# Attention scores as two float32r products on full rows, with operands split once per pair of heads

## The chip, the cores and the metric

The kernel runs on one core of one Trainium2 chip. The metric is device time in microseconds (us) of one execution. A core has a matrix engine (TensorE, PE in the profile; its weight loads are shown apart as PEld), a vector engine (VectorE, DVE), an engine for functions of one input (ScalarE, ACT), GpSimd (POOL) and SyncE (SP), which here only issues transfers. They run beside each other and wait for each other by semaphores. Data lies in SBUF (128 partitions); matrix products land in PSUM, 8 banks of 512 float32 a partition.

## The reference

Attention over 8 batches, 8 heads, 576 positions and 64 features a head, in which only scores within tau of their row's maximum count, then a feed-forward network (FFN) whose activation is a rational function:

```python
scores = scale * np.matmul(q, k.transpose(0, 1, 3, 2))           # 576 x 576 a head
thresh = np.max(scores, axis=-1, keepdims=True) - tau
scores = np.where(scores >= thresh, scores, -1000000000.0)
scores = scores - np.max(scores, axis=-1, keepdims=True)
attn = np.exp(scores)
attn = attn / (np.sum(attn, axis=-1, keepdims=True) + 1e-09)
x = np.matmul(attn, v)                       # heads side by side: 4608 x 512
h = x @ w_in                                 # 512 x 2048
g = (a0 + a1*h + a2*h**2 + a3*h**3) / (1 + |b0|*|h| + |b1|*h**2 + 1e-6)
out = g @ w_out                              # 2048 x 512
```

Which scores count depends on small differences between them, so the scores have to be nearly exact in float32.

## The kernel before

**Units.** Heads are taken in pairs, two times 64 features filling the 128 partitions: 32 pairs (8 batches of 4). 576 positions are four blocks of 128 and a rest of 64. A pair has four full units (one block of 128 queries, both heads) and one short unit (the last 64 queries of both heads in one tile), 160 units in all. For each unit `unit_ops` makes these steps: score product (`f_qk`, lines 642 and 653, TensorE), row maximum (`f_max`, 663, VectorE), threshold (`f_thr`, 667, VectorE), a Prelu with a slope of 2^100 below the threshold (`f_pre`, 680, ScalarE), exponential with its sum (`f_sum`, 684, ScalarE), reciprocal (693 and 697, VectorE), a split of the result into two float16 parts (`f_hi`, 278 or 280; `f_lo`, 708), two DMA transposes issued by SP (720), the product with V (733, TensorE), and the split of its result into `xh` and `xl` (741 or 743, and 747). Since `BY_ACT` is `(1, (0,))`, every unit takes this way; the other branch in the code (`f_exp`, `f_mask`) is not used.

**The score product.** Q and K are in float32, with the features on the partitions. Q is loaded into `QQ` by three transfers and K into `KK` by two (`load_ops`, on SP), two tiles of each in turn, and Q is scaled once a pair ("qs", 278 or 280). Head 0 uses partitions 0 to 63, head 1 partitions 64 to 127. `product` (642) multiplies 64 rows by 512 keys for one head; the last 64 keys of both heads come from 653, over all 128 rows, where blocks of zeros keep the heads apart. In the profile one float32 product of the code is two MATMUL instructions, each with its own weight load.

**The FFN.** `moe_ops` takes 256 rows by 512 hidden columns at a time: a first product in float16 parts (845), ScalarE's scaled copy (854), a chain of VectorE and ScalarE steps for the rational function (859 to 899), and a second product in float32 (906). Its steps of one batch lie between the attention units of the next; those of the last batch follow the last unit.

**Weights.** They arrive as 64-bit words by 32 transfers on the POOL queue (452, 487), each behind a small POOL instruction (400) that waits until the transfer three before it has landed, and are decoded by VectorE and ScalarE (`decode_ops`).

**Order of the work.** Each step is an `Op` with its engine or a choice of engines (`FLEX`), a cost in us, a key (its due place in units), and `Hold`s on buffers. `Plan.order` plays the queues forward with these costs and takes the steps in the order in which they start; that order is the program of each queue. "DMA" stands for SP's queue, "GD" for POOL's. Buffers of one pool are granted in the order of rank. The plan books each buffer, but which physical buffer a step gets is left to the tile pools (`sb.tile(... tag=..., bufs=...)`), which go round in order of request. `POOLS` gives their numbers: "t" are 4 KB work tiles a partition, for weights and the FFN. PSUM banks 0 to 5 hold scores in pairs of banks for the first 25 units (`SINGLE`, one head each), after that banks 0 to 2 hold both heads. While the plan sees TensorE idle early on, it puts in small products that keep it warm (1035).

Of the kernel before, what the change touches and what calls it, by code (L numbers as in the profile page):

```python
# [23 lines left out]
POOLS = {"e": 3, "hi": 3, "pT": 2, "st": 6, "sc": 2, "t": 12, "u": 4, "x": 4, "xr": 1}  # L24
# [4 lines left out]
LEAD, LEAD0 = 2.88, 0.04  # L29
# [10 lines left out]
BY_ACT = (1, (0,))  # L40
# [10 lines left out]
FLEX = {"f1": {"ACT": 0.66, "DVE": 0.345}, "f6": {"DVE": 0.62}, "s1": {"ACT": 0.65, "DVE": 0.396}, "qs": {"ACT": 0.7, "DVE": 0.42},  # L51
        "s2": {"DVE": 0.66},
        "vmax": {"ACT": 0.58, "DVE": 0.68}, "thr": {"DVE": 0.155},
# [24 lines left out]
class Hold:  # L78
# [3 lines left out]
    def __init__(self, pool, uses, sets=None):  # L82
        self.pool, self.uses, self.until, self.sets, self.bank = pool, uses, 0.0, sets, None


class Plan:
# [3 lines left out]
    LAT = {"PE": 0.27, "ACT": 0.28, "DVE": 0.22, "POOL": 0.16, "DMA": 2.3, "GD": 3.4}  # L90
    OWN = {"PE": 0.0, "ACT": 0.15, "DVE": 0.13, "POOL": 0.1, "DMA": 2.3, "GD": 3.4}
# [8 lines left out]
    def pool(self, name, n):  # L100
        self.pools[name] = [0.0] * n
# [8 lines left out]
    def spot(self, h, t):  # L110

        if h.sets is None:
            slots = self.pools[h.pool]
            return (min(slots), None) if slots else None
# [14 lines left out]
    def order(self):  # L129
# [20 lines left out]
        while left:  # L150
# [41 lines left out]
            for h in o.take:  # L192
                if h.sets is None:
                    slots = self.pools[h.pool]
                    slots.remove(min(slots))
                else:
                    h.bank = self.spot(h, t)[1]
                    for i in h.bank:
                        self.banks[i] = None
                if h.pool in line:  # L200
                    line[h.pool].pop()
            for h in o.drop:
# [5 lines left out]
                elif not h.uses:  # L208
                    self.pools[h.pool].append(h.until)
# [18 lines left out]
def masked_attention_rational_ffn(  # L228
# [16 lines left out]
    P = 128  # L245
# [16 lines left out]
    sb = ctx.enter_context(tc.tile_pool(name="sb", bufs=2))  # L262
# [25 lines left out]

    def bank(h):
# [17 lines left out]
    QW = S + REM  # L307
    NQ = 2
    QQs = [const.tile([P, QW], F32, name=f"QQ{i}") for i in range(NQ)]
    KKs = [const.tile([P, QW], F32, name=f"KK{i}") for i in range(NQ)]  # L310
    for t in QQs:
        nc.gpsimd.memset(t[:, NT * P:], 0.0)
    for t in KKs:
        nc.gpsimd.memset(t[0:D, 0:REM], 0.0)
        nc.gpsimd.memset(t[D:P, S:], 0.0)
# [18 lines left out]
    def scale_ops(key, get, up, inv, s, after, tag):  # L334
# [3 lines left out]
        plan.rank = key  # L338

        def f1():  # L340
            sc = small.tile([P, 4], F32, name=f"sc{tag}", tag="sc", bufs=POOLS["sc"])
# [3 lines left out]
        def f2():  # L345

            box["d"] = sb.tile([P, WS], F32, name=f"dg{tag}", tag="u", bufs=POOLS["u"])[:, 0:P]
# [15 lines left out]
        h, hd, hb = Hold("sc", 1), Hold("u", 1), Hold("b", 1, B1)  # L363
# [26 lines left out]
    def decode_ops(i, key, load, hold, dst=None):  # L390
# [13 lines left out]
        def f1():  # L404


            box["w"] = sb.tile([P, WS], F32, name=f"wt{i}", tag="u", bufs=POOLS["u"])
# [21 lines left out]
        l = op("GD", 2.7, key - 2.0, ld, (), [hold])  # L429
# [13 lines left out]
    for i in range(NW):  # L443
        pieces = []
        for c in range(NC):
# [3 lines left out]
            def load(n=n, c=c, i=i):  # L449
                rw = sb.tile([P, 2, WS], F32, name=f"rwi{n}", tag="t", bufs=POOLS["t"]).rearrange("p a b -> p (a b)")  # L450
                rw = words(rw)
# [30 lines left out]
    for f in range(NF):  # L482
        hold = Hold("t", 1)

        def load(f=f):
            rw = words(sb.tile([P, 2, WS], F32, name=f"rwo{f}", tag="t", bufs=POOLS["t"]).rearrange("p a b -> p (a b)"))
# [30 lines left out]
    def load_ops(bp):  # L517
# [3 lines left out]
        before = qk_done.get(bp - NQ, [])  # L521
        KK, QQ = KKs[bp % NQ], QQs[bp % NQ]
        first = bp == 0

        queue, eng = nc.sync, "DMA"

        def ldq():
            queue.dma_start(QQ[0:D, 0:S], qT[bb, pr, :, 0:S])
            queue.dma_start(QQ[D:P, 0:NT * P], qT[bb, pr, :, S + REM:])
            queue.dma_start(QQ[D:P, S:], qT[bb, pr, :, S:S + REM])  # L530

        def ldk():
            queue.dma_start(KK[0:D, REM:], kT[bb, pr, :, 0:S])
            queue.dma_start(KK[D:P, 0:S], kT[bb, pr, :, S:2 * S])

        lq = op(eng, 1.6, p - (4.6 if first else 4.0), ldq, before)
        lk = op(eng, 1.1, p - (4.5 if first else 3.9), ldk, before)
        k_done[bp] = [lk]
        q_done[bp] = [op(FLEX["qs"], 0, p - 1.3, lambda: times(QQ, QQ, qscale), [lq])]

    def load_v_ops(bp):
# [13 lines left out]
        def mx():  # L555
# [4 lines left out]
            else:  # L560
                jk = sb.tile([P, WS], F32, name=f"vj{bp}", tag="u", bufs=POOLS["u"])
                nc.scalar.activation(jk.bitcast(BF16)[:, 0:NT * P + 2 * D], t, AF.Abs, accum_out=vms[bb][:, pr:pr + 1])
# [33 lines left out]
    def x_tile(ck):  # L596
        if ck not in xt:
            tag, n = ("x", POOLS["x"]) if ck[0] == "m" else ("xr", POOLS["xr"])
            xt[ck] = tuple(sb.tile([P, NP, CT], F16, name=f"{tag}{s}{ck[1]}_{ck[2]}", tag=tag + s, bufs=n) for s in "hl")
        return xt[ck]  # L600

    def unit_ops(bp, t):
# [4 lines left out]
        by_act = (bp * (NT + 1) + t) % BY_ACT[0] in BY_ACT[1]  # L607
        heads = (0, 1) if full else (0,)
        QQ, KK = QQs[bp % NQ], KKs[bp % NQ]
# [14 lines left out]
        def f_qk(h2s):  # L624
            if not full:
                h2s = [None]
            s, dst = {}, {}
            for hh in h2s:
                b0, b1 = sh[hh or 0].bank[0], sh[hh or 0].bank[-1] + 1
                s[hh] = ps[:, b0:b1, :].rearrange("p b k -> p (b k)")  # L630
                if hh:

                    s[hh] = s[hh][:, (b1 - b0) * 512 - S:]
                    dst[hh] = s[hh][:, REM:S], s[hh][:, 0:REM]
                else:
                    s[hh] = s[hh][:, 0:S]
                    dst[hh] = s[hh][:, 0:NT * P], s[hh][:, NT * P:S]
                box["s"][hh or 0] = s[hh]

            def product(hh, k0, k1, dst, **kw):  # L640
                r, c0 = (slice(0, P), NT * P) if hh is None else (slice(hh * D, (hh + 1) * D), t * P)
                nc.tensor.matmul(dst, QQ[r, c0:c0 + P], KK[r, k0:k1], **kw)  # L642

            one = dict(start=True, stop=True)
            rests = (S, QW), (0, REM)
            for hh in h2s:

                product(hh, REM, S, dst[hh][0], **one)
            if len(h2s) == 2:

                for hh in h2s:
                    k0, k1 = rests[hh]
                    nc.tensor.matmul(dst[hh][1], QQ[:, t * P:(t + 1) * P], KK[:, k0:k1], **one)  # L653
            elif full:
                product(hh, *rests[hh], dst[hh][1], **one)
            else:
                product(hh, *rests[0], dst[hh][1], start=True, stop=False)
                product(hh, *rests[1], dst[hh][1], start=False, stop=True)

        def f_max(hh):  # L660
            if hh == 0:
                box["st"] = small.tile([P, 8], F32, name=f"st{name}", tag="st", bufs=POOLS["st"])
            nc.vector.tensor_reduce(box["st"][:, hh:hh + 1], box["s"][hh], AX.X, ALU.max, negate=True)  # L663

        def f_thr(h0, h1):
            if by_act:
# [411 lines left out]
```

## Time and profile before

| | us |
|---|---|
| three runs | 1463.76, 1470.2, 1471.97 (median 1470.2) |
| profiled execution | 1455.38 |
| its span, first to last instruction | 1453.6 |
| TensorE busy | 1395.0 |
| VectorE busy | 1230.0 |
| ScalarE busy | 1114.5 |
| POOL busy | 31.5 |

The mean granted clock of TensorE is 0.973 of full speed. Rows of the profile name a line of the kernel, an engine, an operation and its tiles (out<-in, buffer numbers left out), the shapes, and the count. "Mean ns" is the time of one instruction; matrix products overlap, so their pace is read from the distance between starts and not from it. "Idle before" is the time in which the engine stood still just ahead of such an instruction, with what released it ("issue" where the profile shows no cause).

### The profile page before, as it was taken

What the parts mean: (1) busy time and instruction counts of PE and PEld (TensorE: products, weight loads), DVE (VectorE), ACT (ScalarE), POOL (GpSimd) and SP (SyncE); (2) the same over time, 40 slices, a digit from 0 to 9 for tenths busy, and PEclk for the clock granted to TensorE, in tenths of its full rate; (3) what the DMA queues carried; (4) which work ended last, traced back from release to release, by engine and by line L of the source; (5) the groups of instructions that cost most, each with busy time, mean ns of one, the idle gap of its engine ahead of it and who ended that gap; (6) DMA issues with size and microseconds to landing.
All of it is one profiled execution on the core that took longest, in us unless ns stands there. A gap on an engine that the chain in (4) does not pass through costs nothing.

```text
span 1453.6 us, 28174 instructions
## 1 busy us (share of the span) xinstructions
PE 1395.0 (96%) x11040; PEld 873.7 (60%) x11040; DVE 1230.0 (85%) x2197; ACT 1114.5 (77%) x1931; POOL 31.5 (2%) x78
## 2 busy tenths in 40 slices
PE   8788899999999999979999999999999999999998
PEld 6566656665655656546566665566655556565665
DVE  6698898989789889968898989889789979777665
ACT  6698889888878788768767677789787778774553
POOL 3100010000000000000000000000000000000000
PEclk7699999999999999989999999999999999999999
DMA  9888856356454654445435334455455454330000
GB/s 248 198 150 160 151 117 121 81 99 119 93 105 78 119 96 97 92 103 99 87 70 102 78 81 87 94 102 113 89 108 100 89 99 82 81 70 15 16 15 15
DMA packets 391349, 142.37 MB, mean 98 GB/s; under 512 B 357936, under 2 KB 374320, under 8 KB 391216
## 3 DMA queue, kind: packets, MB, share of 16 engines
q1 hardware_dynamic: 386608, 123.80, 44.5%
q0 software_dynamic: 4608, 16.78, 3.9%
q8 instruction: 86, 1.41, 0.4%
q14 instruction: 47, 0.39, 0.1%
HBM read 45.09 MB, written 9.44 MB: 38 GB/s over the span
## 4 chain that ended last, share of the span: by engine, by line
PE 50%; DVE 5%; ACT 1%; issue 1%; DMA 0%; DVEq 0%
PE banks L906 23%; PE banks L845 15%; PE banks L642 5%; PE banks L733 4%; PE banks L653 2%; DVE e L708 1%; DVE st L663 1%; DVE qm L881 0%; DVE rm L899 0%; DVE rm L285 0%; DVE rm L890 0%; DVE qm L896 0%; DVE qm L893 0%; DMA pT<-hi 0%; ACT e L684 0%
## 5 line engine op out<-in xcount | busy, mean ns | idle before, releaser
L906 PE MATMUL banks<-wp,rm 128*128 128x512 f32 x1024 | 478.1, 605 | 7.4 <-DVE rm L899 7.3
L845 PEld LDWEIGHTS <-wi 128*128 128x128 f16 x3456 | 335.3, 99 | 87.2 <-issue 46.2
L845 PE MATMUL banks<-xh,wi 128*128 128x256 f16 x2048 | 364.8, 274 | 7.9 <-ACT hsm L854 7.5
L906 PEld LDWEIGHTS banks<-wp,rm 128*128 128x128 f32 x1024 | 183.5, 192 | 184.1 <-issue 169.7
L845 PE MATMUL banks<-xl,wi 128*128 128x256 f16 x1024 | 280.0, 273 | 0.0
L680 ACT ACTIVATE e<-banks,st 128x576 f32<-128x576 f32 x288 | 205.7, 735 | 76.4 <-DVE st L667 36.0
L663 DVE TENSOR_REDUCE st<-banks 128x1 f32<-128x576 f32 x288 | 213.9, 748 | 50.8 <-PE banks L653 24.4
L642 PE MATMUL banks<-KK,QQ 64*128 64x512 f32 (+3 forms) x784 | 230.2, 557 | 20.3 <-ACT e L680 16.8
L708 DVE SCALAR_TENSOR_TENSOR e<-e,st,hi 128x576 f16<-128x576 f32 x288 | 233.4, 810 | 4.9 <-ACT hi L278 4.1
L684 ACT ACTIVATE e<-e,cf 128x576 f32<-128x576 f32 x288 | 220.5, 773 | 0.2
L278 ACT ACTIVATE hi<-e,st 128x576 f16<-128x576 f32 x242 | 181.4, 768 | 48.0 <-issue 30.7
L733 PEld LDWEIGHTS <-VH 128*64 128x64 f16 x3200 | 124.7, 112 | 72.7 <-issue 68.0
L733 PE MATMUL banks<-pT,VH 128*64 128x128 f16 (+1 forms) x3200 | 150.9, 220 | 14.7 <-DMA pT<-e 14.4
L642 PEld LDWEIGHTS banks<-KK,QQ 64*128 64x128 f32 (+1 forms) x784 | 94.3, 195 | 115.3 <-issue 48.1
L854 ACT ACTIVATE hsm<-banks,hsc 128x512 f32<-128x512 f32 x128 | 86.7, 682 | 65.5 <-PE banks L845 65.3
L733 PE MATMUL banks<-pT,V 128*64 128x128 f16 (+1 forms) x1600 | 136.8, 218 | 0.0
L653 PEld LDWEIGHTS banks<-KK,QQ 128*128 128x128 f32 x432 | 56.7, 191 | 82.6 <-issue 82.6
L884 ACT ACTIVATE Am<-qm,cf 128x1024 f32<-128x1024 f32 (+1 forms) x65 | 73.5, 1131 | 27.4 <-DVE qm L881 27.2
L733 PEld LDWEIGHTS <-V 128*64 128x64 f16 x1600 | 92.1, 113 | 0.0
L893 DVE SCALAR_TENSOR_TENSOR qm<-qm,Am 128x1024 f32<-128x1024 f32 (+1 forms) x65 | 78.0, 1201 | 8.5 <-ACT Am L887 8.4
L899 DVE SCALAR_TENSOR_TENSOR rm<-rm,cf,qm 128x1024 f32<-128x1024 f32 (+1 forms) x65 | 82.1, 1263 | 0.6
L890 DVE SCALAR_TENSOR_TENSOR rm<-rm,cf,hsm 128x1024 f32<-128x1024 f32 (+1 forms) x65 | 82.0, 1261 | 0.4
(115 smaller groups left out, 1559.0 us busy)
## 6 DMA issues: line engine op xcount, KB each, us to landing
KK<-in_kT_dram SPq DMA_DIRECT2D x64, 144.0 KB, 3.0
rwi<-in_w_in_dram POOLq DMA_DIRECT2D x16, 512.0 KB, 6.7
V<-in_v_dram SPq DMA_DIRECT2D x32, 256.0 KB, 3.0
rwo<-in_w_out_dram POOLq DMA_DIRECT2D x16, 512.0 KB, 5.3
out_dram<-om SPq DMA_DIRECT2D x32, 256.0 KB, 2.3
QQ<-in_qT_dram SPq DMA_DIRECT2D x32, 144.0 KB, 2.8
QQ<-in_qT_dram SPq DMA_DIRECT2D x32, 128.0 KB, 2.7
pT<-hi SPq DMA_TRANSPOSE x160, 3.3
```

The source lines that it names most:

```text
L278: nc.scalar.activation(dst, src, AF.Identity, scale=factor)
L642: nc.tensor.matmul(dst, QQ[r, c0:c0 + P], KK[r, k0:k1], **kw)
L653: nc.tensor.matmul(dst[hh][1], QQ[:, t * P:(t + 1) * P], KK[:, k0:k1], **one)
L663: nc.vector.tensor_reduce(box["st"][:, hh:hh + 1], box["s"][hh], AX.X, ALU.max, negate=True)
L680: nc.scalar.activation(ev(hh), box["s"][hh], AF.Prelu, bias=box["st"][:, 2 + hh:3 + hh], alpha=STEEP)
L684: nc.scalar.activation(e, e, AF.Exp, bias=ntau, accum_out=box["st"][:, 4 + hh:5 + hh])
L708: nc.vector.scalar_tensor_tensor(box["lo"][:, c], ev(hh), box["st"][:, 6 + hh:7 + hh], box["hi"][:, c], ALU.mult, ALU.subtract)
L733: nc.tensor.matmul(po[pp, 0:w], V[:, c * P + hh * D:c * P + (hh + 1) * D], rhs, start=c == 0 and n == 0, stop=c == NT and n == 2)
L845: nc.tensor.matmul(d, wi_tile(c, f0 + j, hl), x[:, c, :], start=c == 0 and n == 0, stop=c == NC - 1 and n == 2)
L854: nc.scalar.activation(box["h3"][:, 2 * k:2 * k + 2, sl], psv[:, :, sl], AF.Identity, scale=hsc[:, b2, g:g + 1])
L899: nc.vector.scalar_tensor_tensor(box["r"], box["r"], a0, box["q"], ALU.add, ALU.mult)
L906: nc.tensor.matmul(acc[tt], box["r"][:, o:o + P], wo[f], start=begins and j == 0, stop=ends and j == nb - 1)
```

## The change

- **Scores.** Each pair gets three operand tiles, `QH`, `QL` and `KK`, whose upper 64 partitions and lower 64 partitions hold different parts of the same head, both heads side by side along the free dimension. With q and k split into a part rounded to float32r (h) and the rest (l), `QH` holds qh above and qh below, `QL` holds ql above and zeros below, `KK` holds kh above and kl below. A head's scores are `QH` times `KK` plus `QL` times `KK`, on all 128 rows: qh kh + qh kl + ql kh. Each product is cut at the bank's edge into pieces of 256 and 320 keys, so that a full unit is eight float32r matmuls. A short unit has both heads in one tile, 64 queries each, and eight as well.
- **Splits.** Once a pair: the load of K and of Q into "t" tiles (four transfers on SP), a copy into a second "t" tile as float32r (ScalarE or VectorE) and a subtraction in place (VectorE) for each, then ten SBUF-to-SBUF transfers on the POOL queue that put the parts in place. The scaling of Q is gone; the threshold and the Prelu apply the scale (`scale=qscale`).
- **Maximum.** Beyond the first 25 units, one VectorE instruction takes the maxima of both heads.
- **Small steps.** The threshold and the first half of the reciprocal may also go to ScalarE.
- **Zeros.** The zero blocks are written by VectorE from `ident`, where POOL wrote them.
- **Buffers.** Every tile is made once, and the plan's own choice of buffer (`h.slot`) is the one used. "hi" has 2 buffers for 3, "t" 10 for 12. A score tile's hold counts one use a head where it counted two.
- **Constants.** `LEAD` 3.3 for 2.88, the booked latency of "GD" 2.7 for 3.4, the booked time of a weight transfer 3.3 for 2.7. The loads of a pair are made behind the last unit of the pair before, where they were made ahead of its first; their keys lie 4 units ahead as before.

The core of the diff:

```diff
-POOLS = {"e": 3, "hi": 3, "pT": 2, "st": 6, "sc": 2, "t": 12, "u": 4, "x": 4, "xr": 1}
+POOLS = {"e": 3, "hi": 2, "pT": 2, "st": 6, "sc": 2, "t": 10, "u": 4, "x": 4, "xr": 1}
-LEAD, LEAD0 = 2.88, 0.04
+LEAD, LEAD0 = 3.3, 0.04
-        "vmax": {"ACT": 0.58, "DVE": 0.68}, "thr": {"DVE": 0.155},
+        "vmax": {"ACT": 0.58, "DVE": 0.68}, "thr": {"ACT": 0.24, "DVE": 0.155}, "kh": {"ACT": 0.7, "DVE": 0.42},
...
+                    h.slot = min(slots)[1]
                     slots.remove(min(slots))
...
+    places = {x: [const.tile(f, d, name=f"{x}{i}") for i in range(POOLS[x])] for x, (f, d) in forms.items()}
+    def place(h):
+        return places[h.pool][h.slot]
...
+    QW = 2 * S + REM
+    QHs = [const.tile([P, QW], F32, name=f"QH{i}") for i in range(NQ)]
+    QLs = [const.tile([P, QW], F32, name=f"QL{i}") for i in range(NQ)]
+    KKs = [const.tile([P, QW], F32, name=f"KK{i}") for i in range(NK)]
...
-        lq = op(eng, 1.6, p - (4.6 if first else 4.0), ldq, before)
-        lk = op(eng, 1.1, p - (4.5 if first else 3.9), ldk, before)
-        k_done[bp] = [lk]
-        q_done[bp] = [op(FLEX["qs"], 0, p - 1.3, lambda: times(QQ, QQ, qscale), [lq])]
+        def high(hold, r, w):
+            copy(fr(place(hold)[:, 0:w]), place(r)[:, 0:w])
+        def low(hold, r, w):
+            d = place(r)[:, 0:w]
+            nc.vector.tensor_tensor(fr(d), d, place(hold)[:, 0:w], ALU.subtract)
+        def mvk(part, hold):
+            d, src = KK[part * D:(part + 1) * D], place(hold)
+            nc.gpsimd.dma_start(fr(d[:, 0:S]), fr(src[0:D, 0:S]))
+            nc.gpsimd.dma_start(fr(d[:, S:]), fr(src[D:P, 0:S + REM]))
+        def mvq(d, part, hold):
+            d, src = d[part * D:(part + 1) * D], place(hold)
+            nc.gpsimd.dma_start(fr(d[:, 0:S]), fr(src[0:D, 0:S]))
+            nc.gpsimd.dma_start(fr(d[:, S + REM:]), fr(src[D:P, 0:S]))
+        free_k, free_q = qk_done.get(bp - NK, []), qk_done.get(bp - NQ, [])
+        lk = op("DMA", 1.1, p0, ldk, (), [rk])
+        lq = op("DMA", 1.1, p0 + 0.05, ldq, (), [rq])
+        hk = op(FLEX["kh"], 0, p0 + 1.0, lambda: high(hk_, rk, S + REM), [lk], [hk_])
+        wk = op("DVE", 0.76, p0 + 1.05, lambda: low(hk_, rk, S + REM), [hk], (), [hk_])
+        hq = op(FLEX["kh"], 0, p0 + 1.1, lambda: high(hq_, rq, S), [lq], [hq_])
+        wq = op("DVE", 0.71, p0 + 1.15, lambda: low(hq_, rq, S), [hq], (), [hq_])
+        k_done[bp] = [op("GD", 1.1, p - 1.5, lambda: mvk(0, hk_), [hk] + free_k, (), [hk_]),
+                      op("GD", 1.1, p - 1.45, lambda: mvk(1, rk), [wk] + free_k, (), [rk])]
+        q_done[bp] = [op("GD", 1.1, p - 1.4, lambda: mvq(QH, 0, hq_), [hq] + free_q, (), [hq_]),
+                      op("GD", 1.1, p - 1.35, lambda: mvq(QH, 1, hq_), [hq] + free_q, (), [hq_]),
+                      op("GD", 1.1, p - 1.3, lambda: mvq(QL, 0, rq), [wq] + free_q, (), [rq])]
...
+        def f_qk(hh):
+            if full:
+                o = t * P if hh == 0 else S + 2 * REM + t * P
+                ops = [(x[:, o:o + P], hh * S) for x in (QH, QL)]
+            else:
+                ops = [(x[:, NT * P + h2 * REM:NT * P + h2 * REM + P], h2 * (S + REM)) for h2 in range(2) for x in (QH, QL)]
...
+            edge = 512 - so if so < 512 else 256
+            for c0, c1 in ((0, edge), (edge, S)):
+                for n, (lh, ko) in enumerate(ops):
+                    nc.tensor.matmul(s[:, c0:c1], fr(lh), fr(KK[:, ko + c0:ko + c1]), start=n == 0, stop=n == len(ops) - 1)
...
+                nc.vector.tensor_reduce(box["st"][:, 0:2], box["both"], AX.X, ALU.max, negate=True)
...
-            nc.scalar.activation(ev(hh), box["s"][hh], AF.Prelu, bias=box["st"][:, 2 + hh:3 + hh], alpha=STEEP)
+            nc.scalar.activation(ev(hh), box["s"][hh], AF.Prelu, scale=qscale, bias=box["st"][:, 2 + hh:3 + hh], alpha=STEEP)
```

More of the change, by code (lines that the diff above doesn't have):

```diff
@@ L100, in pool @@
     def pool(self, name, n):
-        self.pools[name] = [0.0] * n
+        self.pools[name] = [(0.0, i) for i in range(n)]
     def op(self, eng, dur, key, fn, after=(), take=(), drop=()):
@@ L597, in x_tile @@
         if ck not in xt:
-            tag, n = ("x", POOLS["x"]) if ck[0] == "m" else ("xr", POOLS["xr"])
-            xt[ck] = tuple(sb.tile([P, NP, CT], F16, name=f"{tag}{s}{ck[1]}_{ck[2]}", tag=tag + s, bufs=n) for s in "hl")
+            xt[ck] = tuple(place(xh_hold[ck])[:, i] for i in range(2))
         return xt[ck]
```

195 lines of the change are left out of this document (79 added, 116 removed).

## The prediction

> **What bounds the kernel now.** I read the busy shares first, then a table of stages, because a share over the whole span averages stages with different limits. The page's first part, then the stages (columns: stretch, its length, busy time and instructions of each engine, granted TensorE clock, DMA share, GB/s):
>
> ```profile
> PE 1395.0 (96%) x11040; PEld 873.7 (60%) x11040; DVE 1230.0 (85%) x2197; ACT 1114.5 (77%) x1931; POOL 31.5 (2%) x78
> ```
>
> ```profile
> core 0: us, PE busy (x) PEld busy (x) DVE busy (x) ACT busy (x) POOL busy (x), PEclk, DMA share, GB/s
> ...
> 80.00:120.00 40.00, 35.24 (x352) 25.42 (x350) 37.37 (x95) 38.87 (x85) 0.98 (x2) 1.00 0.84 144
> 0.00:200.00 200.00, 166.95 (x1400) 122.24 (x1401) 160.00 (x392) 163.01 (x321) 26.57 (x68) 0.85 0.82 173
> 200.00:1300.00 1100.00, 1078.40 (x8839) 660.36 (x8838) 965.40 (x1707) 872.33 (x1503) 4.96 (x10) 0.99 0.49 96
> 300.00:400.00 100.00, 99.49 (x840) 62.79 (x837) 89.70 (x162) 88.66 (x148) 0.00 (x0) 1.00 0.52 100
> 1300.00:1453.00 153.00, 149.68 (x805) 91.08 (x803) 104.56 (x101) 79.17 (x108) 0.00 (x0) 1.00 0.05 14
> ```
>
> There are three stages. From 0 to 200 us, weights are decoded beside the first attention units; from 80 to 120 us ScalarE is busy 38.87 of 40 us and VectorE 37.37, so these two set the pace there. From 200 to 1300 us TensorE is busy 1078.40 of 1100 (98%), VectorE 88%, ScalarE 79%: TensorE bounds. After 1300 us only the FFN is left, with no score product, and TensorE again bounds. The chain that ended last says the same, PE far ahead of the rest:
>
> ```profile
> PE 50%; DVE 5%; ACT 1%; issue 1%; DMA 0%; DVEq 0%
> ```
>
> The change takes work from TensorE in the middle stage and gives work to VectorE, ScalarE, the POOL queue and the start.
>
> **The score products.** One full unit (two heads) and one short unit on the timeline; start, length, engine, line, operation and count. The start of the row behind a unit closes it:
>
> ```profile
> 715.13 1.13 PE L642 MATMUL banks<-KK,QQ 64*128 64x512 f32 x4
> 716.19 0.66 PE L653 MATMUL banks<-KK,QQ 128*128 128x64 f32 x4
> 716.69 0.27 PE L845 MATMUL banks<-xh,wi 128*128 128x256 f16 x1
> 716.80 0.27 PE L845 MATMUL banks<-xl,wi 128*128 128x256 f16 x1
> ...
> 1289.09 1.41 PE L642 MATMUL banks<-KK,QQ 128*128 128x512 f32 x6
> 1290.34 3.65 PE L906 MATMUL banks<-wp,rm 128*128 128x512 f32 x8
> ```
>
> A full unit holds TensorE from 715.13 to 716.69, 1.56 us; a short one 1.25 us. In the middle stage L653 has 424 instructions, four a unit, so 106 full units; the 241 scaled rows of L680 there are two a full unit and one a short one, which leaves about 28 short units:
>
> ```profile
> 200.00:1300.00 1100.00, 70.24 (x424) 55.64 (x424) 0.99 0.49 96
> ```
>
> ```profile
> 200.00:1300.00 1100.00, 171.38 (x241) 0.99 0.49 96
> ```
>
> After the change a unit is eight float32r matmuls of 256 or 320 columns, 2304 columns in all, each with its own weight load. No float32r is in this trace. The f16 rows above start 0.11 us apart for 256 columns, 0.43 ns a column; f32 runs at this pitch:
>
> ```profile
> 1435.95 13.75 PE banks L906 x32
> ```
>
> That is 430 ns for 512 columns, 0.84 ns a column, and an f32 product counts two such instructions (L906 shows two per product of the code). So the unit lies between 2304 x 0.43 = 0.98 us and 1.94 us with one instruction each at f32's pitch. The weight load of 128 f32 columns has a row too:
>
> ```profile
> 716.19 0.52 PEld L653 LDWEIGHTS banks<-KK,QQ 128*128 128x128 f32 x4 [0.76 <-issue]
> ```
>
> Four loads of 0.19 us span 0.52, so they start (0.52 - 0.19) / 3 = 0.11 us apart: eight need 0.88 us, and hide if a load runs beside the matmul before, as L906's do. I take the f16 end and a little for the loads, 1.05 us, since the diff itself splits each operand into a rounded part and a rest: a type that carried all bits would leave no rest, and f32's doubled instructions come from carrying them. Then a full unit saves 0.51 us and a short one 0.20: 106 x 0.51 + 28 x 0.20 = 54 + 6 = 60 us of TensorE in the middle stage (from +59 us added at the f32 end, 40 + 19, to 69 saved at 0.98 us). In the first stage the product's shorter time is worth nothing, since ScalarE and VectorE set it.
>
> The Trainium skill (FP8 and Floating Point Precision, TensorE Precision Notes) says that true fp32 takes four passes through the array and that the reduced form truncates what it reads to the native width. By it float32r would take one pass, and the term would be 69 us in place of 60. The trace agrees on f32 (two instructions of 430 ns, each twice the 0.43 ns a column of f16); no run here shows the reduced form yet.
>
> **VectorE and ScalarE.** Groups by form; columns are busy us, mean ns, idle before:
>
> ```profile
> L663 DVE TENSOR_REDUCE st<-banks 128x1 f32<-128x576 f32 x288 | 213.9, 748 | 50.8 <-PE banks L653 24.4 <-PE banks L642 22.7 <-ACT hsm L854 3.1
> L285 DVE TENSOR_TENSOR rm<-rm,hsm 128x1024 f32<-128x1024 f32 x63 | 76.7, 1217 | 0.2
> L278 ACT ACTIVATE QQ<-QQ,cf 128x640 f32<-128x640 f32 x26 | 21.4, 821 | 4.6 <-DMA QQ<-in_qT_dram 4.5
> L887 ACT ACTIVATE Am<-Am 128x1024 f32<-128x1024 f32 x63 | 66.1, 1049 | 0.6
> L884 ACT ACTIVATE Am<-qm,cf 128x1024 f32<-128x1024 f32 x63 | 72.1, 1144 | 24.6 <-DVE qm L881 24.4
> L667 DVE TENSOR_SCALAR st<-st,cf 128x2 f32<-128x2 f32 x108 | 23.8, 220 | 0.3
> L693 DVE TENSOR_SCALAR st<-st 128x2 f32<-128x2 f32 x128 | 20.8, 163 | 52.3 <-ACT e L684 52.2
> L684 ACT ACTIVATION_READ_ACCUMULATOR e<-e,cf 128x1 f32 x288 | 57.0, 198 | 0.0
> ```
>
> The middle stage has about 27 pairs of heads. VectorE gains two subtractions a pair, of 640 and 576 columns: 1217 ns for 1024 scales (1.04 ns a column plus 150) to 0.82 + 0.75 = 1.57 us, 42 us in all. It loses one fixed part a unit where two maxima become one: 748 - 600 = 148 ns x 106 = 16 us. VectorE 965 becomes about 991. ScalarE loses the scaling of Q (821 ns, 26 of 32 pairs) and gains two plain copies (1049 ns for 1024 gives 0.73 + 0.68 us): +1.41 - 0.67 = 0.74 x 27 = 20 us. Its first pass over the scores now reads its scale from a column too; one such operand is 1144 - 1049 = 95 ns, so 241 x 0.095 = 23 us. ScalarE 872 becomes 915. The threshold and the first half of the reciprocal (220 and 163 ns) may now go to ScalarE, near 0.2 us each by the 198 ns row: 134 units x 2 move up to 50 us, to about 940 and 968.
>
> Over a middle stage of 1050 us, TensorE at 1018 is 97%, VectorE 90 to 94%, ScalarE 87 to 92%. The stretch from 300 to 400 us ran 99/90/89, so this is reachable, not free: I book TensorE at 97% in place of 98%. 1018 / 0.97 = 1050, **50 us less** (61 less with the old share and nothing lost).
>
> **The POOL queue, SP and DMA.** Ten SBUF transfers a pair are new, all on POOL, which carries only weights now; SP loses one of five loads a pair.
>
> ```profile
> KK<-in_kT_dram SPq DMA_DIRECT2D x64, 144.0 KB, 3.0
> rwo<-in_w_out_dram POOLq DMA_DIRECT2D x16, 512.0 KB, 5.3
> ```
>
> ```profile
> q0 software_dynamic: 4608, 16.78, 3.9%
> ```
>
> ```profile
> L487 POOL DMA_DIRECT2D rwo<-in_w_out_dram x16 | 9.4, 588 | 144.8 <-DVE wp L285 70.1 <-ACT e L684 23.0 <-ACT xrh L741 20.5
> ```
>
> Ten issues of 0.59 us are 6 us of POOL a pair. They may start when the pair before last has made its last product and must land before the next pair's first: for the last pair of the trace 44 us.
>
> ```profile
> 1211.66 1.42 PE L642 MATMUL banks<-KK,QQ 128*128 128x512 f32 x6
> ...
> 1255.42 1.13 PE L642 MATMUL banks<-KK,QQ 64*128 64x512 f32 x4
> ```
>
> 6 + 5.3 us to land is covered four times; without that cover each pair would pay 11 us. The bytes (1.5 MB a pair, 48 MB) at q0's rate add 11 points to a DMA share of 0.49. I cost both at nothing in the middle stage.
>
> **The start.** The first product begins at 9.19 us:
>
> ```profile
> 3.06 1.72 POOL L452 DMA_DIRECT2D rwi<-in_w_in_dram  x3
> ...
> 8.34 0.18 POOL L400 TENSOR_SCALAR cf<-rwi 1x1 f32<-1x1 f32 x1 [3.56 <-DMA rwi<-in_w_in_dram]
> ...
> 9.19 1.26 PE L642 MATMUL banks<-KK,QQ 64*128 64x512 f32 x4 [1.99 <-DMA KK<-in_kT_dram]
> ```
>
> Copy 0.73, subtraction 0.82, issues and 3 to 5 us of landing come before it now, and POOL waits at 8.34 for a weight: about 4 us later. The 24 zero fills that go from POOL to VectorE are at most 0.28 us each, 7 us, and run where VectorE waited 6.39 us for its first maximum; I cost them at nothing.
>
> ```profile
> L348 DVE TENSOR_SCALAR dgx<-ident,scx 128x128 f32<-128x128 f32 x8 | 2.3, 282 | 0.5 <-DMA out_dram<-om 0.5
> ```
>
> ```profile
> 10.49 0.76 DVE L663 TENSOR_REDUCE st<-banks 128x1 f32<-128x576 f32 x1 [6.39 <-PE banks L642]
> ```
>
>  In the first stage VectorE then has 7 pairs x 1.57 = 11 us more, ScalarE about 10, where both are at 80% and one stretch is full. I take **+8 us** for the stage (0 to 15). The smaller pools (10 work tiles for 12, 2 for 3) and the places named by the plan I cost at nothing: TensorE's waits add to 22 us of the middle stage, so 22 either way is the most they decide without a new wait.
>
> **Sum.** 1453.6 - 50 + 8 = 1412 us of span; the profiled execution took 1455.4 us, 1.8 above its span, so 1413. The median shown is 1470.2, 14.8 above that execution: **1428 us**.
>
> **Rivals.** (a) All is kept: 69 us off TensorE at the old 98%, start hidden: 70 less, 1400 us; with my 60, 1409. For it speaks the 300-400 us stretch; against it the full first stage. (b) VectorE takes over, which is likelier if the new copies go to it: no stretch of 100 us shows it above 90%. If nothing moves to ScalarE, 991 / 0.93 = 1066 and 991 / 0.90 = 1101 give 1444 to 1479 us, most of it at the long end. Against it: 93% from 80 to 120 us, and the work that may move. (c) The other side, float32r at f32's pitch or with its loads exposed: the gain is gone from 1.56 / 8 = 195 ns an instruction on. At 1.94 us a unit TensorE gets 59 us more, 1137 / 0.97 = 1172, +72 + 8: 1550 us. (d) Transfers late in the first stage: they share POOL's queue with weight loads that wait for buffers.
>
> ```profile
> POOL rwo L487 <- DVE wp L285: 70.1, 3, 44.0
> ```
>
> Two holds such as the longest, 44 us, less some 14 of lead each, are 60 us: 1488. Against it: the plan now orders that queue with both in it. Also POOL's work stretches beside VectorE: the 0.18 us instruction above took 0.52 here.
>
> ```profile
> 29.34 0.88 DVE L582 SCALAR_TENSOR_TENSOR V<-V,sx,VH 128x640 f16<-128x640 f32 x1
> ...
> 29.74 0.52 POOL L400 TENSOR_SCALAR cf<-rwi 1x1 f32<-1x1 f32 x1 [1.75 <-DMA rwi<-in_w_in_dram]
> ```
>
> Stretched so, ten issues are 17 us of 44 a pair and still not late.
>
> The Trainium skill (SBUF — State Buffer, SBUF: two separate sides) warns that a GpSimd-issued DMA gets no descriptors written while VectorE holds the shared port, 620 ns becoming 3100. By that estimate ten issues take 31 us a pair, which still land inside 44 but not when weight loads stand among them, so by this rule (d) would have more than its 0.08. The row agrees in direction (0.18 to 0.52); no row shows an issue that long.
>
> **Chances.** Forecast 0.50, (a) 0.17, (b) 0.16, (c) 0.09, (d) 0.08. Less than 0.5% (1463 to 1478) is about what a measurement can't tell from no change. Faster: the forecast, (a) and a quarter of (b), 0.70; same: most of the rest of (b), 0.11; slower 0.19. The forecast's own range is 1409 to 1447; 1398 to 1480 leaves out (c), (d) and little else.
>
> **What would show it.** Score matmuls starting 0.11 to 0.14 us apart, a unit near 1.05 us; TensorE's busy time down by about 60 to 80 us with the tail unchanged; VectorE at 90 to 94% from 200 us to the end of attention; first product near 13 us; no score matmul waiting for a POOL transfer after the first pairs. I am wrong if units take 1.56 us or more, if TensorE's idle time in the middle exceeds 60 us, or if attention's end moves by less than 20 us.

## The result, and the profile after

The changed kernel takes 1583.75 us (median of four runs, 1568.8 to 1588.1) against 1467.0 before (also of four): a ratio of 1.079, 95% interval 1.069 to 1.089. It is slower by 8%; the forecast was 1428 us, faster. Its profiled execution spans 1567.0 us. Busy shares of the changed kernel, from the page:

```profile
PE 1366.0 (87%) x11272; PEld 962.6 (61%) x11272; DVE 1259.5 (80%) x1993; ACT 1184.0 (76%) x2146; POOL 195.0 (12%) x392
```

TensorE was busy 29 us less (1395 to 1366, and that with 17 us more of the products that only keep it warm), and no other engine took its place: all three are idler than before. So the time went into waiting, and into slower products too, since TensorE's mean granted clock fell from 0.973 to 0.936. The stages (columns as in the prediction):

```profile
0.00:200.00 200.00, 125.05 (x1212) 114.80 (x1213) 127.72 (x306) 129.55 (x281) 43.80 (x97) 0.81 0.97 170
200.00:1300.00 1100.00, 983.14 (x8288) 681.47 (x8288) 929.90 (x1439) 887.31 (x1598) 144.88 (x283) 0.94 0.75 130
1300.00:1567.00 267.00, 257.81 (x1776) 166.36 (x1773) 201.93 (x250) 167.15 (x270) 6.34 (x13) 0.99 0.29 54
```

From 200 to 1300 us TensorE is busy 89% where it was 98%, and the DMA share is 0.75 where it was 0.49. What TensorE waited for (total us, times, longest), first the one such row of the kernel before, then the changed kernel:

```profile
PE banks L733 <- DMA pT<-e: 14.4, 11, 4.1
```

```profile
PE banks L747 <- DMA pT<-e: 115.7, 42, 10.7
PE banks L747 <- DMA pT<-hi: 24.4, 12, 5.6
PE banks L675 <- ACT e L696: 21.6, 31, 5.6
...
PE banks L675 <- DMA QH<-t: 10.1, 1, 10.1
```

The product with V waits for the DMA transposes of the probabilities: 140 us, against 14 before. The score product, which uses the new operands, waits for them at the start only (10.1 and 2.0 us). The chain that ended last now has the transposes in it:

```profile
PE 46%; DMA 21%; DVE 15%; ACT 8%; issue 6%; SPq 1%; POOL 0%; DVEq 0%; ACTq 0%; POOLq 0%
PE banks L911 20%; DMA pT<-e 17%; PE banks L850 14%; PE banks L747 6%; PE banks L675 5%; DVE e L722 3%; ACT e L696 2%; DVE st L681 2%; ACT e L700 1%; ACT hi L278 1%; DVE t L895 1%; DVE st L683 1%; DMA t<-in_kT_dram 1%; DVE t L285 1%; DVE t L901 1%
```

One such wait, close up. First POOL's timeline with the ten transfers of a pair, then SP's with the transposes, then the chain of waits (start, length, what):

```profile
633.36 0.51 POOL L558 DMA_DIRECT2D KK<-t  x1 [36.55 <-DVE t L272]
633.86 0.52 POOL L559 DMA_DIRECT2D KK<-t  x1
...
637.88 0.54 POOL L564 DMA_DIRECT2D QL<-t  x1
```

```profile
635.05 1.25 SPq L734 DMA_TRANSPOSE pT<-hi  x1
636.38 2.49 SPq L734 DMA_TRANSPOSE pT<-e  x1
```

```profile
636.38 12.38 DMA pT<-e
648.81 0.96 PE banks L747 x28
```

A transpose issued at 636.38, in the middle of the ten, lands 12.38 us later. Four-us windows over the same place, with the DMA share second from the right (overlapping packets make it exceed 1):

```profile
634.00:638.00 4.00, 4.00 (x48) 2.83 (x46) 4.00 (x11) 3.67 (x8) 4.00 (x9) 1.00 0.91 175
638.00:642.00 4.00, 3.50 (x32) 2.85 (x30) 3.86 (x7) 3.56 (x5) 0.42 (x1) 1.00 1.75 158
642.00:646.00 4.00, 0.22 (x2) 0.14 (x3) 0.39 (x1) 3.94 (x8) 0.00 (x0) 1.00 1.39 138
646.00:650.00 4.00, 1.19 (x30) 1.06 (x30) 0.20 (x2) 0.57 (x1) 0.00 (x0) 0.59 0.94 66
```

By this count the sixteen DMA engines are full or nearly so from 634 to 650 us; TensorE has nothing it may do from 642 on, and VectorE follows. The granted clock falls as well, and stays low after the wait has ended. A finer window, and the next score product from the chain of waits:

```profile
646.80:653.50 6.70, 4.69 (x45) 3.97 (x45) 2.01 (x5) 0.00 (x0) 0.00 (x0) 0.50 0.47 95
```

```profile
651.16 1.92 PE banks L675 x8
```

At a clock of 0.50 the eight matmuls of a unit take 1.92 us, where most units take 1.06 to 1.08.

Away from such waits the score product does what was forecast. Timeline of one unit:

```profile
659.47 0.31 PE L675 MATMUL banks<-KK,QL 128*128 128x320 f32 x1
659.62 0.28 PE L675 MATMUL banks<-KK,QH 128*128 128x256 f32 x1
659.73 0.28 PE L675 MATMUL banks<-KK,QL 128*128 128x256 f32 x1
659.85 0.28 PE L675 MATMUL banks<-KK,QH 128*128 128x256 f32 x1
659.97 0.28 PE L675 MATMUL banks<-KK,QL 128*128 128x256 f32 x1
```

Starts lie 0.11 to 0.15 us apart, and the chain of waits has 1.06 to 1.08 us for most units of eight.

### The profile page after: what moved, and what is told of

Read it like the earlier page. It is cut to its first block, busy times and chain, and to the rows that moved or that the text cites. A ratio compares the mean times of both kernels' runs of the same rounds, so it can differ in the third digit from the quotient of the medians.

```text
span 1567.0 us, 29732 instructions
## 1 busy us (share of the span) xinstructions
PE 1366.0 (87%) x11272; PEld 962.6 (61%) x11272; DVE 1259.5 (80%) x1993; ACT 1184.0 (76%) x2146; POOL 195.0 (12%) x392
## 3 DMA queue, kind: packets, MB, share of 16 engines
q0 software_dynamic: 30208, 65.03, 23.2%
## 4 chain that ended last, share of the span: by engine, by line
PE 46%; DMA 21%; DVE 15%; ACT 8%; issue 6%; SPq 1%; POOL 0%; DVEq 0%; ACTq 0%; POOLq 0%
PE banks L911 20%; DMA pT<-e 17%; PE banks L850 14%; PE banks L747 6%; PE banks L675 5%; DVE e L722 3%; ACT e L696 2%; DVE st L681 2%; ACT e L700 1%; ACT hi L278 1%; DVE t L895 1%; DVE st L683 1%; DMA t<-in_kT_dram 1%; DVE t L285 1%; DVE t L901 1%
## 5 line engine op out<-in xcount | busy, mean ns | idle before, releaser
L911 PE MATMUL banks<-wp,t 128*128 128x512 f32 x1152 | 541.1, 608 | 3.3 <-DVE t L904 3.2
L850 PE MATMUL banks<-x,wi 128*128 128x256 f16 x3072 | 374.4, 279 | 4.3 <-ACT t L859 3.9
L911 PEld LDWEIGHTS banks<-wp,t 128*128 128x128 f32 x1152 | 210.5, 194 | 205.0 <-issue 194.9
L696 ACT ACTIVATE e<-banks,st,cf 128x576 f32<-128x576 f32 x288 | 233.3, 823 | 33.2 <-DMA pT<-e 27.0
L675 PE MATMUL banks<-KK,QH 128*128 128x320 f32 (+1 forms) x640 | 226.6, 373 | 32.0 <-ACT e L696 21.6
L675 PE MATMUL banks<-KK,QL 128*128 128x320 f32 (+1 forms) x640 | 184.6, 309 | 2.0 <-DMA QL<-t 2.0
L675 PEld LDWEIGHTS banks<-KK,QH 128*128 128x128 f32 x640 | 129.2, 202 | 62.8 <-ACT e L696 34.6
L681 DVE TENSOR_REDUCE st<-banks 128x2 f32<-128x1152 f32 x108 | 145.8, 1350 | 25.3 <-PE banks L675 24.3
L859 ACT ACTIVATE t<-banks,hsc 128x512 f32<-128x512 f32 (+1 forms) x192 | 106.1, 576 | 70.5 <-PE banks L850 68.0
L675 PEld LDWEIGHTS banks<-KK,QL 128*128 128x128 f32 x640 | 130.1, 203 | 17.7 <-issue 17.6
```

The source lines that it names most:

```text
L675: nc.tensor.matmul(s[:, c0:c1], fr(lh), fr(KK[:, ko + c0:ko + c1]), start=n == 0, stop=n == len(ops) - 1)
L681: nc.vector.tensor_reduce(box["st"][:, 0:2], box["both"], AX.X, ALU.max, negate=True)
L696: nc.scalar.activation(ev(hh), box["s"][hh], AF.Prelu, scale=qscale, bias=box["st"][:, 2 + hh:3 + hh], alpha=STEEP)
L850: nc.tensor.matmul(d, wi_tile(c, f0 + j, hl), x[:, c, :], start=c == 0 and n == 0, stop=c == NC - 1 and n == 2)
L859: nc.scalar.activation(box["h3"][:, 2 * k:2 * k + 2, sl], psv[:, :, sl], AF.Identity, scale=hsc[:, b2, g:g + 1])
L911: nc.tensor.matmul(acc[tt], box["r"][:, o:o + P], wo[f], start=begins and j == 0, stop=ends and j == nb - 1)
```

## Experiments

Theory A: the transfers load the DMA engines, the transposes land late, and TensorE, whose order is fixed, stands still behind them. Theory B: buffers, order and the new VectorE and ScalarE work cost the time, and the transfers are hidden. Ratios are to the kernel before on the same chip, with the 95% interval.

**Smaller pools alone** (e1b).

```diff
-POOLS = {"e": 3, "hi": 3, ..., "t": 12, ...}
+POOLS = {"e": 3, "hi": 2, ..., "t": 10, ...}
```

> The kernel before with only the smaller pools of the change: 10 work tiles for 12, 2 'hi' tiles for 3. Theory A (the SBUF transfers fill the DMA engines in bursts and make the transposes late): within 1% of the kernel before, 1455 to 1480 us. Theory B (the loss comes from buffers, order and the new VectorE and ScalarE work, the transfers are hidden): slower by 20 us or more.

1467.0 us, 1.0055 (1.002 to 1.009). The pools cost half a per cent.

**The transfers alone** (e1): the kernel before with those pools, and behind the loads of K:

```diff
+            if bp:
+                src = KKs[(bp - 1) % NQ]
+                for i, part in ((0, 0), (0, 1), (1, 0), (1, 1), (2, 0)):
+                    d = DST[i][part * D:(part + 1) * D]
+                    nc.gpsimd.dma_start(fr(d[:, 0:S]), fr(src[0:D, 0:S]))
+                    nc.gpsimd.dma_start(fr(d[:, S:]), fr(src[D:P, 0:S]))
```

> As the kernel before with the smaller pools, and with ten extra SBUF-to-SBUF transfers of 64 x 576 float32 a pair on the POOL queue, issued behind the loads of K, from the K tile of the pair before into scratch tiles that nobody reads (from the second pair on). Nothing else is added and the order of the other queues is the same. Theory A: 80 to 140 us slower than without them, with score-times-V products waiting for transposes (over 100 us in all, against 14). Theory B: within 15 us of the run without them, since nobody waits for these transfers.

1597.6 us, 1.094 (1.088 to 1.099): 131 us more than without, for transfers that no engine's work waits for. TensorE's waits for transposes in this kernel, 97 us where over 100 were expected:

```profile
PE banks L740 <- DMA pT<-e: 71.4, 32, 15.4
PE banks L740 <- DMA pT<-hi: 25.8, 12, 6.6
```

From the trace's issue and landing of each of the 320 transposes ("in flight" is at any time between the transpose's issue and its landing):

```
                       mean us to land   over 5 us
kernel before                 3.50           15
smaller pools (e1b)           3.50           17
change                        4.77           91
idle transfers (e1)           4.75           84
   129 with a transfer in flight   6.56
   191 without                     3.52
```

The median hides this (3.3 before, 3.4 after). Of e1's 84 late transposes 79 lie beside a transfer. A late one has more time to meet a transfer, but the split holds when only transfers already in flight at its issue are counted: 7.35 us for 84, 3.82 us for 236.

**The change without its transfers** (e2): `mvk` and `mvq` return at once from the third pair on.

```diff
+            if bp >= NK:
+                return
```

> The changed kernel with the transfers into QH, QL and KK made for the first two pairs of heads only. It leaves the placing of the operands out for the other 30 pairs, whose scores are computed from those of the first two; all loads, copies, subtractions, products and the order of the work stay. Theory A: about 1410 to 1440 us, transposes land in 3 to 5 us, and TensorE waits for them under 25 us. Theory B: 1550 us or more.

1411.3 us, 0.967 (0.962 to 0.971). Its stages:

```profile
200.00:1240.00 1040.00, 1015.13 (x8930) 705.08 (x8929) 990.43 (x1523) 941.14 (x1700) 11.34 (x18) 0.99 0.53 105
```

TensorE is at 98%, VectorE at 95%, ScalarE at 90% over 1040 us. It still waits 35 us for transposes, more than the 25 expected. Theory B falls: with all the new engine work and order in place the kernel is 51 us faster than the kernel before beside it (1462.5), and the transfers cost about 170 us (1583.75 - 1411.3 by the medians; 0.112 of the time before, some 165 us, by the ratios).

The page of e2 also shows how the time was lost:

```profile
PE 1315.7 (93%) x11272; PEld 929.0 (66%) x11272; DVE 1253.7 (89%) x1993; ACT 1178.5 (84%) x2146; POOL 42.9 (3%) x92
```

TensorE has the same 11272 instructions as in the change, and they take 1315.7 us in place of 1366.0, at a mean granted clock of 0.975 in place of 0.936. Of the 159 us between the two profiled spans (1407.7 and 1567.0), 109 are idle time of TensorE and 50 are the same products running longer. With its transfers out of the way the change takes 79 us off TensorE's busy time (1395.0 to 1315.7), and the lower clock hides 50 of them.

**The type** (e4): plain float32 on both sides of the ten transfers (one of four such lines).

```diff
-            nc.gpsimd.dma_start(fr(d[:, 0:S]), fr(src[0:D, 0:S]))
+            nc.gpsimd.dma_start(d[:, 0:S], src[0:D, 0:S])
```

> The changed kernel with the ten transfers a pair as plain float32 on both sides in place of float32r, still on the POOL queue. Theory A in the form 'the bytes do it': same as the changed kernel, 1570 to 1590 us. Theory A in the form 'transfers of the float32r type are slow': the burst of about 10 us a pair shrinks to about 5 (the pace of the weight loads), the queue's share falls from 23% to about 13%, and the time falls to 1450 to 1510 us. Theory B: no difference.

1599.8 us, 1.091 (1.081 to 1.100). Plain float32 is no faster, and the queue's share is 19.9%, not 13%; the type is not it.

**The queue** (e5): e1 with SP's queue for the idle transfers, in plain float32.

```diff
-                    nc.gpsimd.dma_start(fr(d[:, 0:S]), fr(src[0:D, 0:S]))
+                    nc.sync.dma_start(d[:, 0:S], src[0:D, 0:S])
```

> As the kernel before with smaller pools plus ten idle transfers a pair, but issued from SP's hardware queue as plain float32. If the bytes fill the 16 DMA engines whichever queue they come from: 1570 to 1610 us, as with POOL's queue (1597.6). If POOL's software queue is what holds the transposes up: 1470 to 1510 us.

1682.1 us, 1.149 (1.144 to 1.154), worse than both expected. The transposes land as quickly as before (mean 3.55 us); they are issued late instead. SP's timeline:

```profile
714.79 0.60 SPq L535 DMA_DIRECT2D KK<-in_kT_dram  x1
715.43 0.59 SPq L540 DMA_DIRECT2D DST<-KK  x1
...
721.21 0.59 SPq L541 DMA_DIRECT2D DST<-KK  x1
721.91 1.38 SPq L727 DMA_TRANSPOSE pT<-hi  x1
```

Ten issues hold the queue 6.4 us in front of a transpose, on top of five loads. The hardware queue trades a late landing for a late issue.

The run shows one thing more. Beside one of these transfers in flight a transpose landed in 3.96 us (68 of them), without one in 3.44; beside POOL's transfers it was 6.56 and 3.52. The transfers themselves landed in 3.1 us in the median where POOL's took 5.8, and took 6.0 us of the sixteen engines a pair where POOL's took 9.3. So by this run the late landing goes with POOL's queue and not with the bytes alone. What in that queue does it no run shows (POOL also issues faster, every 0.50 us against 0.64), nor what these transfers would cost on a hardware queue that issues no transposes.

**Spread, with nobody waiting** (e6): two idle transfers placed in the program at each of the pair's five score products (`f_mv` issues the two).

```diff
         def f_qk(h2s):
+            if h2s[0] == 0 and bp < NBP - 1:
+                f_mv()
```

> The same ten idle transfers a pair on POOL's queue, but two at each of the pair's five score products in place of ten in a row. If the length of the burst counts (ten transfers hold the DMA engines some 10 us, and the transposes of one or two units behind them): the loss of 130 us shrinks to 50 or less, 1470 to 1515 us. If the sum of DMA time counts: 1580 to 1605 us.

1598.9 us, 1.095 (1.088 to 1.103): as in a row. But they did run in a row. POOL waits for the load of K and for no score product, so it issues all ten one behind the other:

```profile
649.65 0.51 POOL L667 DMA_DIRECT2D DST<-KK  x1 [29.77 <-DMA KK<-in_kT_dram]
...
656.45 0.56 POOL L668 DMA_DIRECT2D DST<-KK  x1
```

From a pair's first issue to its last it is 6.1 us in the median, against 6.0 in e1; only the first seven pairs were spread, over 10 to 46 us. The run says nothing on a burst's length.

**Spread in the change** (f1): each two transfers also wait for one score product of the pair before.

```diff
+        gate = [qk_unit.get((bp - 1, i), []) for i in range(4)]
...
-                      op("GD", 1.1, p - 1.45, lambda: mvk(1, rk), [wk] + free_k, (), [rk])]
+                      op("GD", 1.1, p - 1.45, lambda: mvk(1, rk), [wk] + free_k + gate[0], (), [rk])]
```

> The changed kernel with its five pairs of transfers held back, one pair of transfers behind each of the first four score products of the pair before. If the burst counts: 1440 to 1500 us, TensorE waits for transposes under 60 us in all. If the sum counts: 1560 to 1590 us.

1554.4 us, 1.063 (1.058 to 1.069): 29 us better by the medians, in neither range, with 129 us of waits for transposes. Here too the ten mostly run in a row, because POOL comes to them when the pair's copies are ready, and by then nothing holds them apart:

```profile
667.14 0.51 POOL L559 DMA_DIRECT2D KK<-t  x1 [31.50 <-ACT t L270]
...
671.90 0.51 POOL L565 DMA_DIRECT2D QL<-t  x1 [0.21 <-issue]
```

First issue to last is 5.8 us in the median, against 5.7 in the change. So neither run tests whether a long burst costs more than the same transfers spread out, and what made f1 faster stays open.

**Fewer** (e7): four idle transfers a pair (edit against e1).

```diff
-                for i, part in ((0, 0), (0, 1), (1, 0), (1, 1), (2, 0)):
+                for i, part in ((0, 0), (0, 1)):
```

> The kernel before with smaller pools and only four idle SBUF transfers a pair in place of ten. If each transfer delays the transposes by its own share: 0.4 of the 130 us, 1505 to 1530 us. If only a long burst hurts: under 1485 us.

1502.5 us, 1.029 (1.022 to 1.036): 36 us over e1b, just under the first range and less than 0.4 of 131 (52). The four are issued within 1.7 us in the median, so the length of the burst may count for something; this run can't part it from the sum.

**From HBM** (e8), and the same held back (e9, with the last line); edits against e1:

```diff
-                    nc.gpsimd.dma_start(fr(d[:, 0:S]), fr(src[0:D, 0:S]))
+                    nc.gpsimd.dma_start(d[:, 0:S], kT[bb, pr, :, 0:S])
...
+                nc.gpsimd.tensor_scalar(cf[0:1, 15:16], src[0:1, S - 1:S], 1.0, 1.0, ALU.mult, ALU.mult)
```

> The ten idle transfers a pair on POOL's queue with the same shape (64 x 576 float32) and place, but read from K in HBM in place of SBUF. If any bytes on the DMA engines delay the transposes alike: 1570 to 1605 us. If it is reading SBUF that costs: 1480 to 1540 us.

1664.0 us, 1.137 (1.130 to 1.145), but it says nothing on the source: with no load of K to wait for, POOL ran ahead and issued them all in the first 600 us. e9 holds them back by one small POOL instruction that reads the K tile of the pair before:

> The ten idle transfers a pair from HBM again, now held back like those from SBUF by one small POOL instruction that reads the K tile of the pair before (without it POOL ran ahead and issued them all in the first 600 us). If any bytes delay the transposes alike: 1570 to 1610 us. If reading SBUF is what costs: 1480 to 1540 us.

1573.0 us, 1.076 (1.068 to 1.085): 106 us over e1b, 131 from SBUF. Transfers of POOL's queue from either source delay the transposes; by these two runs reading SBUF accounts for some 25 us of the 131.

**Slack in TensorE's order** (g1, g4, control g0). The plan is told that what SP issues is seen later, so that the product with V stands later in TensorE's order:

```diff
-    LAT = {..., "DMA": 2.3, "GD": 2.7}
+    LAT = {..., "DMA": 5.3, "GD": 2.7}     # g1; 8.3 in g4; the kernel before with 3.8 in g0
```

> The changed kernel with the plan told that a transfer of SP's queue is seen 5.3 us after its issue in place of 2.3, so that the products with V stand 3 us later in TensorE's order; transfers as in the change. If TensorE stands still because its fixed order has no slack for a late transpose: 1470 to 1530 us, waits for transposes under 80 us. If the DMA engines themselves are the bound: 1560 us or more.

> The changed kernel with that time at 8.3 us (2.3: 1584 us, 5.3: 1519 us). If the missing slack is nearly all of the loss: 1440 to 1490 us. If the DMA engines' own time sets a floor: 1505 to 1530 us.

> Control: the kernel before with SP's transfers booked as seen after 3.8 us in place of 2.3, nothing else. If the later booking helps only where transposes are late: 1450 to 1475 us, no difference from before. If it is a gain of its own: under 1445 us.

g1 1519.0 us, 1.037 (1.029 to 1.045); g4 1480.7 us, 1.016 (1.011 to 1.021); g0 1456.4 us, 0.999 (0.995 to 1.004). With the same transfers, 6 us of slack give back about 100 of the 170 us. TensorE waits 72 us for transposes in g1. TensorE's waits in g4:

```profile
PE banks L675 <- ACT e L696: 58.5, 39, 8.3
...
PE banks L747 <- DMA pT<-e: 1.4, 4, 0.5
```

The wait for transposes is gone (1.4 us; they still take 4.51 us in the mean), and TensorE waits for ScalarE to empty the score banks, 58.5 us where it was 21.6. Longer held buffers would explain that; it was not tried. The control shows no gain of its own for 1.5 us in the kernel before; 6 us without the transfers was not run.

**Without transfers between partitions** (f2, g2, g3). K and Q are loaded from HBM to both halves of the partitions, rounded and subtracted there, through one tile `RR` for both; 9 work tiles for 10.

```diff
+            for h in range(2):
+                nc.sync.dma_start(RQ[h * D:(h + 1) * D, :], qT[bb, pr, :, :])
...
+            copy(fr(QH[:, 0:S]), RQ[:, 0:S])
...
+            nc.vector.tensor_tensor(fr(KK[D:P, 0:2 * S]), RK[D:P, :], KK[D:P, 0:2 * S], ALU.subtract)
```

> The changed kernel without SBUF transfers: K and Q are loaded from HBM to both halves of the partitions (four loads of 64 x 1152 a pair on SP), rounded and subtracted in place on the engines, 9 work tiles for 10. VectorE gets about 1.4 us a pair more than in the change, ScalarE about 1.2 (38 and 45 us in all). If the transfers were the only loss: 1415 to 1450 us. If loads from HBM hold the transposes up as SBUF transfers do (1.2 MB a pair in two parts): 1480 to 1530 us.

> The version without SBUF transfers (loads from HBM to both halves, splits on the engines) with that time at 3.8 us in place of 2.3. It ran 1440 us with 48 us of TensorE waiting for transposes. If slack takes most of that: 1405 to 1430 us; if VectorE at 90% is what holds it: 1435 to 1450 us.

> The version without SBUF transfers with that time at 5.3 us. At 2.3 it ran 1440 us, at 3.8 it ran 1419 us with 15 us of waits for transposes left. If slack has done what it can: 1410 to 1430 us.

f2 1440.4 us, 0.985 (0.980 to 0.990); g2, with 3.8 us in the plan, 1419.3 us, 0.970 (0.963 to 0.976); g3, with 5.3, 1427.3 us, 0.980 (0.975 to 0.984). g2's shares:

```profile
PE 1327.5 (94%) x11344; PEld 938.7 (66%) x11344; DVE 1292.3 (91%) x2061; ACT 1219.6 (86%) x2203; POOL 32.6 (2%) x72
```

g2 beats both kernels: loads of twice the bytes, and 33 us more of VectorE than in the change (1292.3 against 1259.5), cost less than the transfers did. These loads come by SP's queue, and the transposes land in 3.66 us in the mean.

## Why the prediction was wrong, by its steps

**What held.** *Score products*: 1.05 us a unit booked, 1.07 measured. *VectorE and ScalarE*: groups of the changed kernel,

```profile
L696 ACT ACTIVATE e<-banks,st,cf 128x576 f32<-128x576 f32 x288 | 233.3, 823 | 33.2 <-DMA pT<-e 27.0 <-issue 3.9 <-DVE st L711 0.7
L681 DVE TENSOR_REDUCE st<-banks 128x2 f32<-128x1152 f32 x108 | 145.8, 1350 | 25.3 <-PE banks L675 24.3 <-ACT st L705 0.3
L554 DVE TENSOR_TENSOR t<-t,t 128x640 fp32r<-128x640 f32 x32 | 26.1, 817 | 2.8 <-ACT t L270 2.8
L688 ACT ACTIVATE st<-st,cf 128x2 f32<-128x2 f32 x62 | 23.5, 380 | 11.9 <-DVE st L681 11.8
```

the first pass went from 735 to 823 ns (+95 booked), the joint maximum saves 146 ns a unit (148), the subtraction takes 0.82 us (0.82). Only the threshold on ScalarE was mis-sized, 380 ns for about 200. *The middle stage*: 1050 us at 97% was booked; e2 took 1040 at 98%, with VectorE at 95%, so rival (b) falls too. The last product with V starts at 1304 us before, at 1253 in e2 and at 1412 in the change.

**What failed: "I cost both at nothing in the middle stage".** The step asked whether the transfers themselves would be late, and they never were after the start. It did not ask what they make late. With them 91 transposes took over 5 us to land, where 15 did before; TensorE waited 140 us for transposes in place of 14, its clock fell, and about 170 us were lost. The prediction's own sign for this, idle time of TensorE above 60 us in the middle, stands at 117 us (1100 - 983.14). The bytes were also mis-sized: at the pace of the weight loads they were to add 11 points of DMA share, and POOL's queue took 23.2% where it took 3.9%:

```profile
q0 software_dynamic: 30208, 65.03, 23.2%
```

19 points are 302 us of all sixteen engines, 9.4 us a pair, for transfers booked by a number that I did not hold against the transposes already there. The profile of before had the warning: 320 transposes of 3.3 us to landing, a DMA share near one half, and TensorE already waiting for "DMA pT<-e" here and there, 14 us in all, so that its order held no slack for a later one.

**The start**: first product forecast near 13 us; it came at 25.98 (9.19 before). SP issues the first K load at 6.71 us, behind nine transfers of V (3.37 before), and it lands at 12.21. POOL's first transfer waited 9.73 us, in the end for ScalarE's copy of that K, and QH's transfers, issued from 16.01 us on among weights, took 8 to 9 us to land.

```profile
25.98 0.64 PE L675 MATMUL banks<-KK,QH 128*128 128x320 f32 x1 [10.11 <-DMA QH<-t]
```

```profile
13.31 0.53 POOL L558 DMA_DIRECT2D KK<-t  x1 [9.73 <-ACT t L270]
```

17 us in place of 4; e2 has the same late start (26.25) and is still 51 us faster than before, so this is no main part of the loss.

**Rivals.** (c) float32r at f32's pitch did not happen. (d) named the right transfers and the wrong victim: it let the score product wait for them. The rule of the Trainium skill (SBUF — State Buffer, SBUF: two separate sides) behind it speaks of the time of a whole transfer that waits for its descriptors, where the prediction took it for the time of an issue. No run here decides it: POOL's issues in the change take 526 to 537 ns in the mean beside a busy VectorE and at most 0.77 us, but how much of the 4.1 to 8.0 us to landing (medians by tile) is such waiting no view shows. That float32r takes one pass, as the prediction read the Trainium skill (FP8 and Floating Point Precision, TensorE Precision Notes), agrees with the starts: 0.11 us for 256 columns, f16's pace.

**What stays open.** Why ten transfers a pair cost about 170 us in the change and idle ones 131 in the kernel before. By the profiles TensorE's idle time grew by 109 and 84 us and the time of the same products by 50 and 41; why the change waits longer was not tried, and the faster score product may leave less to do beside a late transpose. Whether a long burst costs more than spread transfers, since no run spread them. What in POOL's queue makes a transpose beside it land late. And g4's 68 us over e2 by the profiles are 27 of idle time and 41 of busy time, 28 of these in products that only keep TensorE warm; what the rest is these runs do not show.

## What to carry to other kernels

A transfer that nobody waits for still has a price: add its engine time to the DMA share, ask which queue it comes from, and look at which transfer on the shared engines has the least slack before a fixed order. Medians of landing times hide it; look at means, at those in flight together, and at the queue's sequence. If an operand must lie in two places, loading it twice from HBM and spending a little more VectorE time can be cheaper than moving it across partitions by the software queue (g2 against g4, 1419 and 1481 us), and the order of the waiting engine should be planned with the landing time that the loaded DMA engines really give.

## What the runs showed of the hardware beyond that

- DMA transposes landed in 6.56 us beside a transfer of the software queue and in 3.52 without (e1); beside the same transfers issued from their own hardware queue in 3.96 and in 3.44 without, but behind 6.4 us of issues (e5).
- A float32r matmul of 256 columns with its own 128 x 128 weight load starts every 0.11 to 0.12 us (659.62 to 659.97 in the change), so its loads hide beside the products.
- TensorE stood still for 5.9 us until 648.81, and the granted clock was 0.50 from 646.8 to 653.5 us, so that it was still low when the products began again. Over the whole execution such stretches made the same TensorE instructions take 1366.0 us in the change and 1315.7 in e2: the late transposes cost nearly half as much again as the waiting itself (50 us on 109).
